# A linear-attention and mixture-of-experts kernel: the written-out order of its steps replaced by another, and more places for the experts' products among the Sinkhorn steps

## The chip, the cores and the metric

The kernel runs on one core of one Trainium2 chip. A time is the device time of one execution in microseconds (us); the figure for a kernel is the median of its runs. A profiled execution gives besides a trace, whose span runs from the first to the last instruction.

## The reference

Two computations follow one another. The first is gated linear attention over batch 4, 8 heads, 768 tokens, head size 48, in float32:

```python
for t in range(S):
    state = alpha[:, :, t, :, None] * state + np.einsum('bhd,bhe->bhde', k[:, :, t], v[:, :, t])
    y[:, :, t] = np.einsum('bhd,bhde->bhe', q[:, :, t], state)
```

Its output, as x of 3072 tokens by 384, goes through a mixture of eight experts (F = 1024) whose weights come from eight rounds of Sinkhorn normalization over all tokens:

```python
P = np.exp(logits - logits.max())          # logits = x @ w_gate
for _ in range(8):
    P /= P.sum(1, keepdims=True) + 1e-09
    P /= P.sum(0, keepdims=True) + 1e-09
    P *= N / E
for e in range(E):
    out += P[:, e:e + 1] * (np.maximum(x @ w1[e], 0.0) @ w2[e])
```

Every token's routing weight so depends on the logits of all tokens, and the Sinkhorn steps can begin only when the last chunk of attention is done. The experts' products need only x.

## The kernel before, in words

**Precision and tiles.** Each matrix of the experts is kept as two float16 parts, high and low; a product is three passes on PE, the matmul engine (lines with PASSES). In `moe_tile` a tile is T tokens (128 or 256) of one expert e: eight columns of the first layer, each of nine products into a tile `ps1` (in traces `ps<-xT,w`), evacuated by ACT (`h[0]`, ReLU) and DVE (`h[1]`, the low part); then for each 128 tokens 24 products of 128x384 (`ps<-w,h`), whose result ACT copies to `r` and SP, the queue engine, writes to DRAM as `raw`. Four PSUM buffers (psm) hold these results, so PE can run four columns ahead of the evacuation. Experts 0 to 2 are handled in this way, beside the attention; their tiles are called the filler. Experts 3 to 7 follow in a later stage with another algorithm (`first`, `second`), which starts when the filler is used up.

**Attention.** The tokens of a batch are cut into chunks of 128 and units of 256 (two chunks). The first four chunks (0 to 3, of batch 0) go through `direct_chunk`: PE transposes alpha, k and q; then for L = 1, 2, 4, 8, 16, 32, 64 small products of 32x16 and larger give the scores of level L (`psl`), DVE copies them under a mask into `A32` (rows `A<-odd,psl`), and `merge` multiplies keys and queries by decays (`T<-T,D`) and the decays among themselves (`D<-D`). This last multiplication is on DVE, or on POOL (GpSimd) where `lop[0]` is set. All other units first go through `attn_block`, which forms products of q and k of 16 tokens on POOL (`tmp_0`, `tmp_1`, ...), sums them on DVE (`AB<-tmp`), and writes the result to DRAM and back; then `attn_decays`, and `attn_chunk` for each of its two chunks (`Tk`, `Tq`, `decq`, `deck`, `psl`, `A`). Both kinds of chunk end in `attn_tail`: `psy` (the output), `pskn` and `pss` (the new state `ST`), the scaled x (`xT`) and the logits (`psg`, `lg`).

**Expert weights.** `load_expert` loads w1 and w2 of experts 0 to 2 into buffers that later hold x, ACT squares them with a sum (`w<-xT`), PE adds over partitions (`pst_w`), and ACT and DVE make the two halves; with `lop[0]` set, POOL makes the low half. `load_late` does the same for experts 3 to 7 through one staging buffer (`w1f`, then `w2f` in the same memory), a generator with a yield between its steps; the squares go to `junk`.

**Order.** The engines run the instructions in the order in which they are written (`keep_in_program_order`), PE, ACT, DVE, POOL and SP each in its own. That order is set by two strings: START for the first part of the kernel, and UNIT, which is repeated for every further unit with its numbers shifted. In them `f` emits filler worth 0.45 us of PE time (`fill`), `c3` the next step of chunk 3, `b3` the next step of the block of unit 3, `d3` its decays, `w1` the next step of loading expert 1, `g` one step for the gate's weights. A capital letter sets `lop[0]` for the step, so its multiplications go to POOL. A step that would come too early is put off (`early_`). Where there is no filler yet, `f` emits nothing.

**Sinkhorn.** `sinkhorn` is a generator. It takes the maximum of all logits (`gm` on DVE, `pst_gg` on PE, `oneg_gg` on DVE, `pso_gg` on PE, back on DVE), the exponential on ACT, and eight rounds of DVE work with one product over partitions each (`pssk`). Between its steps the caller fills in filler, and from the third step on a step of `load_late` for expert 3. The rest of the filler follows in the loop after it, with a step of `load_late` for every 2.0 us of filler as soon as no tile of expert 0 is left.

Of the kernel before, what the change touches and what calls it, by code (L numbers as in the profile page):

```python
# [25 lines left out]
def tile_gla_moe(ctx: ExitStack, tc: tile.TileContext, q, k, v, alpha, wg, w1, w2, out):  # L26
# [3 lines left out]
    E, _, FF = w1.shape  # L30
# [6 lines left out]
    NTT = NT // P  # L37
    NP = H // 2
    DP = 64
    START = 'c0 C0 f c0 f c0 c1 f c0 f C1 f f c0 f f f f f f f f f f f f f f f f f f f C0 f f f f f f f f f f f f f f f f f f f f f f f f f f f f f f f f f f f f f f f f f f f f f f f f f f f f f f f f f f f f f f f W0 f f f f f f f f f f f f f f f f C2 f f f f f f f c0 W0 f f f f f f f f f f f f f f f f f f f f f f f f f W0 f f f c1 f f f f f f f f f b2 f f f f f f f f f f f f f f f C2 f f f f f f f f f f f f f f f f f f f f f f f f f f f f f f c1 f f f f f f f f f W0 f f f f f f f f f f f f f f f f f f f f f f f f f f f f f f f f f f f f f f f f f w0 c1 f C0 f f f f f f f f f f f w0 f f f f f f f f f w0 f f f f f f f f f f C1 f w0 f f f f f f f f f f f f f f f f f f f f f f f f f f f f f f f f f f f f f f f f f f f f f f f c0 f f f f f f f f f f f f f f f f f f f f f f f f f f f f f f f f f f f f f f f f f f f f f f f f f f f f f f f f f f f f f f f f f f f f f f f f f f f f C1 f f f f f f f f f f f f f W1 f f f f f f f f f f f W1 f f f f f f f f f f f f f f f f f f f f f f f f f d2 f f f f f f f f f f f f f f W0 f f f f f f f f f f f f f f f f f f f f f f f f f f f f f f f f f f f f f f f f f f f C1 f f f f c0 f f f f f f f f f f b2 f f f f f f f f f f f f f f f f f C1 f w0 f f f f f f f f f f C2 f f f f f f f f f f f f f f f f f f f f f f f f f f B2 f f f f f f f f f f f f f f f f B3 f f f f f f f f f f f f f f f f f f f f f f f f f f f f f f f f f f f f f f f f f f f f f f f f f f f f f f f f f f f f f f f f f f c1 f f f f f f f f f f f f f f f f f f f c3 f f f f f f f f f f f f f f f C1 f f f f f f f f f f f f f f f f f f f f f f f f f f f b2 f f f f f f f f f f f f f f f f f f f f f f f f f f f f f f f f f f f f f f C2 f f f f f f g f f f f f f f f f f f f f f c0 B2 f f f f B2 f f f f f f c2 f f f f f f B2 f f f f f f f f f f f f f f f f C3 f f f f b2 f B3 f f f f f f f f c3 f f f f f f f f f f f f f f f f f W0 f f f f f f f f f b2 f f f f c1 f f f f f f f f f f f f c0 f f f f f f f f f f f f f f f f f c2 f w1 f f f f c3 f f f f f f f f f f f f f f f f f f f f f f f f f c2 f f f f f f f f f f f f f f f f f f f f f f f f f f w2 f f f f f f f f f f f f f f f c2 f f C3 f B2 f f f f f f W1 f f f f f B2 f f f f f f f f f f f f f f f f f W0 f c2 f f f f f f f f f f f f f f f f f f W0 f f f f f f f f f f f f f f f g f f f f f f f f f f f f w0 f f f f f f f f f f f f f f f f f C3 W0 f C2 f f f f f f W0 f f f f C3 f f f f f f f f f f B2 f W1 f f f f f f f f f f f f f f C3 f f f f f f f f f f f f f f C2 f f f f f f f f f f f f f f f f f f f f f f f f f f f C2 f f f f f f f f f f f f f f f f f f f f f f f f f f f f f w2 f f f f f f f f f f f f f f f f f f f f f f f f f f f f f f f f f f w2 f f f f b3 f f f f f f f f f B3 f f f b2 f f f f f f f f f f f f f f f f f f f f f f f f f d3 f f f f f C1 f f f f f b2 f f f f f f f f f f f f B2 f f f f f f f f f f W0 f f f f f f f f f f f f f f f w2 f f g f f f f f f f f f f f f f f f f f f f f f C3 f f f f f f f f f f f f f f f f f f f f f f f f f f f w1 f f f f f f f f f f f b3 f f f f f f f f f f f f w1 f f f c3 f f f c3 f f f f f f f f w1 f f f f f f f C3 f f f f f f f f f W1 f f c4 f f f f f b2 f f f f f f W1 f f f f f w1 f f f f f f f f f f W1 f f f w1 c4 f f f B3 f f B3 f f f f f f f f f f f f f f f f f f f f f f f f f f f f f f f f f f f f f f f f f f f f f f f f f f f f f f f f f f f f f f f f f f f f f f f f f f f f f f f f f f f f f w1 f f f f f f c4 f f f f f f f f f f c4 f f f f f f f f f f f f w2 f f f f c4 f f f f f f f w2 f f f f f f f f f f f f f f f f f f f f f f f f f f f f f f f f f f f f f f f f f f w2 W1 f f C2 w2 f f w2 f f f f f f f f f f f f f f f f f f f f f f f f f f f f f f f f w2 f f w1 f f f f b3 f f c3 b3 f f f f f f f f f f f f f f f c5 f f f f f f f f w2 b3 f B3 f f c6 b4 f f f f f f f B3 f b3 f f f B3 f f f f w2 f B3 f f f f f f f f f w2 c5 f f f f f f c5 f f c5 f f c4 f f f c5 f f f f w2 f f f f f f c5 f f f f f f w2 f w2 f f f w1 f f f b3 f f f b4 f f f f f f f f f f f f f f f f f B4 b4 f f f f B4 f f b4 f b4 f f f f f f B4 f f f f f f f f f f f f b4 f f f c6 B4 f f f B4 f f c6 b4 f c8 b4 f f f b4 f f f f f f b4 f c7 b5 f c6 c7 b4 f f f f c6 f f f f f f c6 f d4 f f f f f f f f f f f f f f c7 f f f c8 f c7 f f B5 c7 b5 f f f c7 f b5 f B5 B5 b5'.split()  # L40
    UNIT = 'f f f f f f f f f f f f f f f f c1 f f c0 f B1 f f f f f f f f c1 f f f f f f f f b1 f f B1 f f b1 f f b1 f f b1 f f b1 f B1 f f f f f f c0 f f B2 f f f f f f f f c1 c0 f f B1 f f c1 f c1 f f f f f d1 f f c1 f f f f f f f f f c2 f f f b2 f f f f f f c2 f f f f f f f f f f b2 b2 B2 B2 b2 f c0'.split()
    NA = 3

    pin = tc.keep_in_program_order
# [24 lines left out]
    def tr(out_, in_, idn):  # L69
# [15 lines left out]
                            fill=0.0, base=0, channel_multiplier=1)  # L85
# [46 lines left out]
    def spread(one, nm):  # L132

        n = one.shape[1]
        ps = psa.tile([P, 512], F32, tag="psa", name=f"pso_{nm}")
        mm(ps[:, :n], ones[0:1, :], one)
        g = sm.tile([P, n], F32, tag=f"all{n}", name=f"all_{nm}")
        VE.tensor_copy(g, ps[:, :n])
        return [g[:, i:i + 1] for i in range(n)]
# [594 lines left out]
    def fill(us):  # L734
        owed[0] += us
        while owed[0] > 0 and filler:
            e, gen, n = filler[0]
            if n == FT and e not in ready:
                break
            try:  # L740
                owed[0] -= next(gen)
                filler[0][2] += 1
            except StopIteration:
                filler.pop(0)
        owed[0] = min(owed[0], 0.0)
# [124 lines left out]
    def sinkhorn():  # L870
        gm = sm.tile([P, 1], F32, tag="gm", name="gm")
        VE.tensor_reduce(gm, lg, axis=AX.XY, op=ALU.max)
        gg, = spread(top(gm, None, "gg"), "gg")
        lm = mp.tile([P, NTT, E], F32, tag="lm", name="lm")
        VE.tensor_scalar(lm, lg, gg, None, op0=ALU.subtract)
        SE.activation(PR, lm, AF.Exp)
        for it in range(N_SINKHORN):
            rs = sm.tile([P, NTT], F32, tag="rs", name=f"rs_{it}")
            VE.tensor_reduce(rs, PR, axis=AX.X, op=ALU.add)
            VE.tensor_scalar_add(rs, rs, EPS)  # L880
            ri = sm.tile([P, NTT], F32, tag="ri", name=f"ri_{it}")
            VE.reciprocal(ri, rs)
            VE.tensor_mul(PR, PR, ri.unsqueeze(2).to_broadcast([P, NTT, E]))
            yield
            ps = psa.tile([P, 512], F32, tag="psa", name=f"pssk_{it}")
            mm(ps[:, :NTT * E], ones, PR.rearrange("p t e -> p (t e)"))
            cs = sm.tile([P, E], F32, tag="cs", name=f"cs_{it}")
            VE.tensor_reduce(cs, ps[:, :NTT * E].rearrange("p (t e) -> p e t", e=E), axis=AX.X, op=ALU.add)

            VE.tensor_scalar(cs, cs, EPS, float(E) / NT, op0=ALU.add, op1=ALU.mult)  # L890
            ci = sm.tile([P, E], F32, tag="ci", name=f"ci_{it}")
            VE.reciprocal(ci, cs)
            VE.tensor_mul(PR, PR, ci.unsqueeze(1).to_broadcast([P, NTT, E]))
        VE.tensor_mul(PR, PR, p2t.unsqueeze(2).to_broadcast([P, NTT, E]))
# [93 lines left out]
    filler[1:] = sorted(filler[1:], key=lambda x: x[0])  # L988
    w3_ = load_late(NA)
    advance(w3_, 1)  # L990
    for n, _ in enumerate(sinkhorn()):
        fill(2.8 if n else 4.0)
        if n > 1:
            advance(w3_, 1)
    while filler:
        if all(e for e, *_ in filler):
            advance(w3_, 1)
        fill(2.0)
    advance(w3_, 99)
    early.close()  # L1000
    attn_ps.close()
# [161 lines left out]
```

## Time and profile before

| | us |
|---|---|
| median of 3 runs | 1732.25 (1730.5 to 1732.73) |
| profiled execution, device time | 1735.68 |
| its span, first to last instruction | 1734.0 |

The mean granted clock of PE in the profiled execution is 0.975. The program has 46403 instructions, 19984 of them matmuls. In rows of a timeline the first number is the start in us from the start of the span, the second the duration, and a bracket gives the idle time of the engine before it and what ended that. A row with xN merges N neighbouring instructions of the same kind; its duration is then from the first start to the last end or the sum, short waits included. PE, DVE, ACT, POOL and SPq name the engines (SPq is SP's queue of DMA issues).

### The profile page before, as it was taken

How to read it: one execution, taken by the hardware profiler on the slowest of the kernel's cores; microseconds unless marked ns; L12 is line 12 of the kernel's file. 1: busy time of each engine (PE TensorE's matmuls, PEld its weight loads, DVE VectorE, ACT ScalarE, POOL GpSimd, SP SyncE). 2: the span in 40 equal slices, each digit the busy share in tenths (PEclk: the TensorE clock that was granted, in tenths of full speed). 3: DMA queues.
4: the chain of work that ended last, by engine and by line, in shares of the span. 5: the costliest groups of instructions: out<-in, count | busy, mean ns of one | idle time of the engine just before them, and what ended most of it. 6: DMA issues, size and time to landing. Idle time of an engine off the chain costs nothing.

```text
span 1734.0 us, 46403 instructions
## 1 busy us (share of the span) xinstructions
PE 1650.9 (95%) x19984; PEld 1420.5 (82%) x19984; DVE 1221.1 (70%) x2992; ACT 796.8 (46%) x1592; POOL 290.9 (17%) x262
## 2 busy tenths in 40 slices
PE   5679999999999999999999999999999999999999
PEld 4556767777777777776899999999999999999998
DVE  5767767666656766355577878888788867786666
ACT  3456433334333434334465545554555445544443
POOL 2424245435533633000000000000000000000000
PEclk7679999999999999999999999999999999999999
DMA  7153422442243133021202020202020201000001
GB/s 178 37 124 87 105 63 60 100 100 61 59 101 89 48 90 73 24 61 55 69 24 70 29 65 25 69 28 58 28 65 29 51 2 38 2 1 20 29 29 38
DMA packets 149501, 98.91 MB, mean 57 GB/s; under 512 B 108464, under 2 KB 139440, under 8 KB 149296
## 3 DMA queue, kind: packets, MB, share of 16 engines
q1 hardware_dynamic: 149296, 95.95, 21.2%
q8 instruction: 156, 2.56, 0.6%
q14 instruction: 49, 0.40, 0.1%
HBM read 67.63 MB, written 28.30 MB: 55 GB/s over the span
## 4 chain that ended last, share of the span: by engine, by line
PE 78%; DVE 15%; ACT 3%; issue 2%; POOL 1%; DMA 1%; SPq 0%; ACTq 0%; DVEq 0%; POOLq 0%
PE ps L67 49%; PE ps2x L67 12%; PE ps2v L67 3%; PE ps2z L67 3%; DVE h L58 3%; PE ps2y L67 3%; PE psy L67 2%; PE psl L67 2%; DVE hf L58 2%; DVE w L58 1%; ACT h L58 1%; DVE acc L58 1%; DVE decq L58 1%; DVE AB L58 1%; DVE deck L58 1%
## 5 line engine op out<-in xcount | busy, mean ns | idle before, releaser
L67 PE MATMUL ps<-xT,w 128*128 128x256 f16 (+1 forms) x6984 | 806.9, 273 | 16.2 <-DVE h L58 11.5
L67 PEld LDWEIGHTS <-w 128*128 128x128 f16 x6984 | 676.5, 98 | 99.4 <-issue 18.4
L67 PEld LDWEIGHTS <-h 128*128 128x128 f16 x6768 | 588.0, 98 | 118.4 <-issue 9.4
L58 ACT CAST h<-hf 128x896 f16<-128x896 f32 x240 | 224.8, 937 | 337.6 <-DVE hf L58 227.6
L58 DVE TENSOR_TENSOR h<-hf,h 128x896 f16<-128x896 f32 x240 | 261.5, 1089 | 165.5 <-ACT h L58 164.0
L67 PE MATMUL ps<-w,h 128*128 128x384 f16 x1728 | 297.1, 327 | 0.5 <-DVE h L58 0.4
L67 PE MATMUL ps2x<-w,h 128*128 128x192 f16 x2880 | 267.7, 246 | 7.6 <-DVE ps2z L58 5.5
L58 DVE TENSOR_TENSOR hf<-hf 128x128 f32<-128x128 f32 x960 | 235.3, 286 | 39.5 <-ACT hf L58 30.8
L58 DVE SCALAR_TENSOR_TENSOR h<-ps,h 128x256 f16<-128x256 f32 (+1 forms) x296 | 115.6, 411 | 140.9 <-ACT h L58 140.3
L58 ACT ACTIVATE h<-ps 128x256 f16<-128x256 f32 (+1 forms) x296 | 110.3, 377 | 164.1 <-PE ps L67 164.1
L58 ACT ACTIVATE hf<-ps 128x512 f32<-128x512 f32 x240 | 142.4, 593 | 54.1 <-PE ps L67 54.1
L58 POOL TENSOR_TENSOR tmp<-qt,kt 128x768 f32<-128x768 f32 (+1 forms) x80 | 133.2, 1670 | 126.9 <-DVE qt L58 72.7
L58 ACT COPY r<-ps 128x384 f32<-128x384 f32 x72 | 34.4, 479 | 158.5 <-PE ps L67 144.1
L58 DVE TENSOR_REDUCE AB<-tmp 128x16 f32<-128x768 f32 (+2 forms) x90 | 80.7, 903 | 33.5 <-POOL tmp L58 33.3
L67 PE MATMUL ps2v<-w,h 128*128 128x192 f16 x720 | 70.2, 248 | 0.0
L58 ACT COPY A<-psl 16x128 f32<-16x128 f32 (+3 forms) x164 | 52.5, 327 | 37.5 <-PE psl L67 25.3
L67 PE MATMUL ps2y<-w,h 128*128 128x192 f16 x720 | 69.2, 246 | 0.0
L67 PE MATMUL ps2z<-w,h 128*128 128x192 f16 x720 | 69.2, 246 | 0.0
L58 DVE SCALAR_TENSOR_TENSOR acc<-ps2x,pe,acc 128x192 f32<-128x192 f32 x120 | 49.2, 410 | 1.8 <-PE ps2x L67 1.8
L67 PE MATMUL psl<-T 48*32 48x16 f32 (+2 forms) x1472 | 24.1, 219 | 27.4 <-DVE T L58 10.9
L67 PEld LDWEIGHTS psl<-T 48*32 48x32 f32 (+1 forms) x1472 | 20.7, 139 | 31.8 <-DVE T L58 12.4
L58 ACT ACTIVATE w<-w2f,s_w 128x768 f16<-128x768 f32 x35 | 32.6, 933 | 30.5 <-DVE w2f L58 29.1
(186 smaller groups left out, 1325.5 us busy)
## 6 DMA issues: line engine op xcount, KB each, us to landing
raw<-r SPq DMA_DIRECT2D x72, 192.0 KB, 1.9
ri<-raw SPq DMA_DIRECT2D x72, 192.0 KB, 2.4
w1f<-in_moe_w_dram SPq DMA_DIRECT2D x20, 384.0 KB, 7.0
w2f<-in_moe_w_dram SPq DMA_DIRECT2D x5, 1536.0 KB, 7.0
VN<-in_v_dram SPq DMA_DIRECT2D x48, 96.0 KB, 3.0
xT<-in_moe_w_dram SPq DMA_DIRECT2D x6, 768.0 KB, 4.6
out_dram<-acc SPq DMA_DIRECT2D x24, 192.0 KB, 2.0
qt<-in_q_dram SPq DMA_DIRECT2D x10, 384.0 KB, 4.7
```

Source lines behind the costliest of these rows:

```text
L58: r = f(*a, **k_)
L67: tc.keep_in_program_order(nc.tensor.matmul(out_, lhsT, rhs, start=start, stop=stop, **k_))
```

## The change

Two things are replaced. First, both strings START and UNIT. The new START has 1972 steps where the old one has 1996, the new UNIT 131 where the old one has 132; the steps of chunks, blocks, decays and weights are the same in number, the number of `f` differs (1783 and 1807, 102 and 103), and which of them are capitals changes. According to its author the order was found by a planner that now takes PE's clock at the front as half. Second, the Sinkhorn generator yields the amount of filler that it wants, has two more yields in its first part, and the loop behind it takes 2.4 instead of 2.0 us of filler per step. The number of yields before the steps of `load_late` set in is raised by the two, so these begin in the same round.

```diff
-    START = 'c0 C0 f c0 f c0 c1 f c0 f C1 f f c0 f f f
...
-    UNIT = 'f f f f f f f f f f f f f f f f c1 f f c0 f B1 f f
...
+    START = 'c0 C0 C0 C0 f C1 f c0 f f f f f f f f C1 f f f
...
+    UNIT = 'f f f f f f f f f f f f f f c1 f f c0 f f f f f f f B1
...
         VE.tensor_reduce(gm, lg, axis=AX.XY, op=ALU.max)
-        gg, = spread(top(gm, None, "gg"), "gg")
+        yield 1.2
+        one = top(gm, None, "gg")
+        yield 0.8
+        gg, = spread(one, "gg")
...
             VE.tensor_mul(PR, PR, ri.unsqueeze(2).to_broadcast([P, NTT, E]))
-            yield
+            yield 2.8 if it else 4.0
...
-    for n, _ in enumerate(sinkhorn()):
-        fill(2.8 if n else 4.0)
-        if n > 1:
+    for n, us in enumerate(sinkhorn()):
+        fill(us)
+        if n > 3:
             advance(w3_, 1)
     while filler:
         if all(e for e, *_ in filler):
             advance(w3_, 1)
-        fill(2.0)
+        fill(2.4)
```

Three places show what moves. The first is ACT behind the Sinkhorn rounds. `r_22` and `r_23` are copies of the second layer's results of the tile of expert 1 at token 2816, `h_2_2560` the evacuations of the next tile, `junk,w2m` the squares of expert 3's w2, which wait for the load of `w2f`. Before:

```order
L58 COPY r_22_11483<-ps_1_2816_0_11456 128x384
L58 COPY r_23_11514<-ps_1_2816_1_11489 128x384
L58 ACTIVATE junk,w2m_11517<-w2f_11487 128x768 x2
L58 ACTIVATE h_2_2560_11520<-ps_2_2560_0_11522 128x256
L58 ACTIVATE h_2_2560_11520<-ps_2_2560_1_11534 128x256
L58 ACTIVATE junk,w2m_11517<-w2f_11487 128x768 x2
L58 ACTIVATE h_2_2560_11520<-ps_2_2560_2_11548 128x256
```

And now:

```order
L58 COPY r_22_11483<-ps_1_2816_0_11456 128x384
L58 COPY r_23_11514<-ps_1_2816_1_11486 128x384
L58 ACTIVATE h_2_2560_11517<-ps_2_2560_0_11519 128x256
L58 ACTIVATE h_2_2560_11517<-ps_2_2560_1_11531 128x256
L58 ACTIVATE junk,w2m_11543<-w2f_11494 128x768 x2
L58 ACTIVATE h_2_2560_11517<-ps_2_2560_2_11546 128x256
L58 ACTIVATE h_2_2560_11517<-ps_2_2560_3_11558 128x256
```

The first two evacuations of the tile now stand ahead of the squares. On PE, 24 products of the tile of expert 1 at token 2560 that stood behind `pso_gg` now stand ahead of `pst_gg` or between the two.

The second place is POOL in a repeated unit, at chunk 2 of batch 2. `deck`, `A` and `Tk` belong to the chunk, `tmp_2_2_..` to the block of a later unit. Before:

```order
L58 TENSOR_TENSOR ST_119<-ST_120,dtot_0_5649 48x4x48 x2
L58 TENSOR_TENSOR deck_2_2_6621<-Tk_2_6606,suf_130 128x256
L58 TENSOR_TENSOR A_2_6623<-an_1_6438,mask 128x8x8x16
L58 TENSOR_TENSOR tmp_2_2_54_6649<-qt_2_6454,kt_2_6455 128x768
L58 TENSOR_TENSOR Tk_2_6606<-Tk_2_6606,k_2_1_6525 128x512
L58 TENSOR_TENSOR tmp_2_2_55_6786<-qt_2_6454,kt_2_6455 128x384
```

And now:

```order
L58 TENSOR_TENSOR ST_119<-ST_120,dtot_0_5647 48x4x48 x2
L58 TENSOR_TENSOR deck_2_2_6567<-Tk_2_6552,suf_130 128x256
L58 TENSOR_TENSOR A_2_6569<-an_1_6219,mask 128x8x8x16
L58 TENSOR_TENSOR Tk_2_6552<-Tk_2_6552,k_2_1_6523 128x512
L58 TENSOR_TENSOR tmp_2_2_54_6776<-qt_2_6383,kt_2_6384 128x768
L58 TENSOR_TENSOR tmp_2_2_55_6799<-qt_2_6383,kt_2_6384 128x384
```

The first product of the block has moved behind `Tk`, which may start only after the chunk's `psl` on PE has read the old value.

The third place is DVE in the front, from the first scores of chunk 2 (`A_0_2`) to x of chunk 0 (`xT_0`), on which the first tile of filler waits. `AB_123` are the sums of the block of unit 2, `qt_2` and `al_2` its merges. Before:

```order
L58 TENSOR_TENSOR A_0_2_945<-psl_2_912,same 128x256
L58 TENSOR_TENSOR T_2_768<-T_2_768,D_0_2_766 128x2x256
L58 TENSOR_REDUCE AB_123<-tmp_0_2_0_894 128x16
L58 TENSOR_TENSOR qt_2_587<-qt_2_587,al_2_589 128x768
L58 COPY_PREDICATED A_0_2_945<-odd,psl_2_912 128x128
L58 TENSOR_TENSOR T_2_768<-T_2_768,D_0_2_979 128x2x128x2
L58 TENSOR_REDUCE wgm<-wgf 128x1
L58 TENSOR_TENSOR xT_0_82<-ys_0_879,xT_0_79 128x3x128
```

And now, from the first sum of the block on:

```order
L58 TENSOR_REDUCE AB_123<-tmp_0_2_0_822 128x16
L58 TENSOR_TENSOR T_1_368<-T_1_368,D_0_1_884 128x2x4x64
L58 TENSOR_TENSOR qt_2_475<-qt_2_475,al_2_477 128x768
L58 TENSOR_REDUCE wgm<-wgf 128x1
L58 TENSOR_REDUCE AB_123<-tmp_0_2_1_1026 128x8
L58 TENSOR_TENSOR qt_2_475<-qt_2_475,al_2_477 128x8x48
L58 TENSOR_TENSOR al_2_477<-al_2_477 128x8x48
L58 TENSOR_REDUCE AB_123<-tmp_0_2_2_1034 128x4x2
L58 COPY_PREDICATED A_0_2_928<-odd,psl_2_895 128x128
L58 TENSOR_TENSOR D_0_2_1072<-D_0_2_962 128x128
L58 TENSOR_TENSOR T_2_768<-T_2_768,D_0_2_962 128x2x128x2
L58 TENSOR_TENSOR xT_0_82<-ys_0_831,xT_0_79 128x3x128
```

Two more sums of the block and the merges between them have moved ahead of chunk 2's second level and of `xT_0`. Its loads (`qt`, `al`, `kt`) are issued ahead of those of chunk 2 where they stood behind them. Among the D merges of `merge`, POOL now has the first two of chunk 0 and of chunk 3 (128x256 and 128x128) and the first of chunk 1, where it had those of chunk 2.

More of the change, by code (lines that the diff above doesn't have):

```diff
@@ L42, in tile_gla_moe @@
+    UNIT = 'f f f f f f f f f f f f f f c1 f f c0 f f f f f f f B1 f f f f f b1 f f f f f f f B1 f f f f b1 B1 f f b1 f f B1 b1 f f b1 f f f f f c0 f c1 f f f f f f B2 c1 f f f f f f c0 f f c1 f f f f f d1 f f f f c1 c2 f f f f f f f f c1 f f f f c2 c0 f f f f f f f f b2 f f f f f B2 f b2 f B2 f B2 b2'.split()
     NA = 3
```

3 lines of the change are left out of this document (1 added, 2 removed).

## The prediction, made before the changed kernel ran

> **What bounds the kernel now.** I read the page first, then the busy time by stage, then PE's waits by stage, and last the timelines at the places where those waits stand. The page says that PE, the matmul engine, is busy for 95% of the span:
>
> ```profile
> span 1734.0 us, 46403 instructions
> PE 1650.9 (95%) x19984; PEld 1420.5 (82%) x19984; DVE 1221.1 (70%) x2992; ACT 796.8 (46%) x1592; POOL 290.9 (17%) x262
> ```
>
> So the end can only move by what PE idles and by what it does at a lowered clock. The table by stage (columns: length, busy time and instructions of PE, of its weight loads, of DVE, ACT and POOL; then granted clock, DMA share, GB/s) says where that is:
>
> ```profile
> 0.00:130.00 130.00, 80.74 (x2308) 64.49 (x2309) 82.41 (x193) 55.81 (x127) 41.38 (x70) 0.73 0.47 113
> 130.00:330.00 200.00, 187.84 (x2416) 142.63 (x2416) 141.65 (x268) 93.66 (x241) 84.50 (x66) 0.99 0.35 88
> 330.00:740.00 410.00, 405.84 (x5274) 310.00 (x5267) 255.38 (x496) 155.07 (x420) 165.01 (x127) 1.00 0.28 69
> 740.00:840.00 100.00, 94.12 (x718) 70.97 (x717) 54.75 (x149) 39.44 (x83) 0.00 (x0) 0.98 0.27 73
> 840.00:1734.00 894.00, 882.41 (x9292) 832.38 (x9289) 686.93 (x1889) 452.87 (x723) 0.00 (x0) 1.00 0.12 35
> ```
>
> The front, up to 130 us, has 49.3 us of PE idle time (130 less 80.74) at a mean clock of 0.73. The next 200 us have 12.2 us idle, the repeated units (330 to 740) 4.2 us, the Sinkhorn stage (740 to 840) 5.9 us at 0.98, and the rest 11.6 us. The rest is code that the change does not touch. PE's work itself is the same products in another order, so the four earlier stages hold all that can be gained.
>
> What PE waits for in the front (total us, times, longest):
>
> ```profile
> PE psl L67 <- DVE T L58: 10.9, 7, 3.8
> PE psl L67 <- DVE A L58: 8.2, 7, 2.0
> PE psl L67 <- issue: 6.7, 3, 3.8
> ```
>
> These are the chunk chains: DVE's merges (T) and masked copies (A), each of which PE's next small products need. The 6.7 us put down to "issue" are waits for nothing that the profile shows, and I expect the change to leave them. In the repeated units little is left:
>
> ```profile
> PE psl L67 <- DVE decq L58: 2.5, 5, 0.5
> PE ps L67 <- DVE h L58: 1.7, 1, 1.7
> ```
>
> **The Sinkhorn stage.** It has four waits that I can name:
>
> ```profile
> PE ps L67 <- DVE h L58: 2.8, 1, 2.8
> ...
> PE pssk L67 <- DVE PR L58: 1.0, 1, 1.0
> PE pst_gg L70 <- DVE gm L58: 1.0, 1, 1.0
> ...
> PE pso_gg L67 <- DVE oneg_gg L58: 0.4, 1, 0.4
> ```
>
> The first Sinkhorn steps run in series: DVE's maximum gm, PE's transposition of it, DVE's maximum of that, PE's spreading. In the program before, nothing stands between them on PE. The two new yields let `fill` put products there: in the new order 24 products of the experts stand ahead of pst_gg, and six between it and pso_gg. At 0.11 us or more each (4.09 us for 36 smaller ones, in a row below) six take at least 0.68 us and cover the 0.37; so 0.96 + 0.37 = 1.33 us go. The 1.03 us in front of the last pssk go too: there PE has two columns of nine products between two pssk before, and three now, while DVE's chain between them is unchanged.
>
> The largest item is the wait of 2.76 us for h. Its cause is not DVE. PE's own rows (idle time in brackets):
>
> ```profile
> 793.61 4.09 PE L67 MATMUL ps<-xT,w 128*128 128x256 f16 x36
> 800.47 5.76 PE L67 MATMUL ps<-xT,w 128*128 128x256 f16 x36 [2.76 <-DVE h L58]
> ```
>
> ACT's row just ahead of it, and the queue's row of the load for which ACT waits:
>
> ```profile
> 797.78 0.84 ACT L58 ACTIVATE junk<-w2f 128x768 f16<-128x768 f32 x1 [3.44 <-DMA w2f<-in_moe_w_dram]
> ```
>
> ```profile
> 790.93 0.38 SPq L58 DMA_DIRECT2D w2f<-in_moe_w_dram  x1
> ```
>
> ACT runs in order. It reached the squares of the w2 load at 794.34, the load issued at 790.93 released them only at 797.78, and h stood behind them. PE ran on until its four buffers were full. Besides that, the 36 products after the wait took 5.76 us where the 36 before it took 4.09, and the clock fell:
>
> ```profile
> 800.00:803.00 3.00, 2.53 (x16) 1.96 (x16) 1.42 (x5) 2.81 (x8) 0.00 (x0) 0.71 0.00 0
> ```
>
> The loss is 2.76 + (5.76 - 4.09) = 4.43 us. With 2.4 in place of 2.0 us per step, the squares come two evacuations of h later (the ACT rows in the section on the change); the load is released by the same DVE work as before and lands at the same place. By hand: PE then has two more columns of about 1.02 us (4.09 / 4) before it blocks, so 2.76 shrinks to about 0.8, a second short wait of some 0.4 follows behind the other two squares, and an idle time that short should keep the clock. I take 1.2 us left and 3.2 gained. Sum of the stage: 1.33 + 1.0 + 3.2 = **5.5 us**; bounds 2.4 (the load's wait merely moves) and 6.8 (all four gone).
>
> **The repeated units.** In each one PE waits 0.50 us for decq:
>
> ```profile
> 449.29 0.68 PE L67 MATMUL psl<-decq,deck 48*64 48x64 f32 x16 [0.50 <-DVE decq L58]
> ```
>
> The cause stands on POOL and DVE:
>
> ```profile
> 446.87 1.99 POOL L58 TENSOR_TENSOR tmp<-qt,kt 128x768 f32<-128x768 f32 x1
> ```
>
> ```profile
> 447.12 2.02 DVE L58 TENSOR_TENSOR decq<-Tq,pre 128x256 f32<-128x256 f32 x1
> ```
>
> DVE's decq of 128x256 began at 447.12 and took 2.02 us, ending with POOL's tmp that began at 446.87 and ended at 448.86. In the new unit POOL's product Tk, which waits for the psl group itself, stands ahead of that tmp, so nothing is on POOL when decq runs. Also twelve products more stand between PE's transposition and psl, so decq is early anyway. Of 2.5 + 1.7 = 4.2 us I take **3.3**; all of it is the lower bound of the time. The upper bound is no gain: psy of the unit's second chunk now follows its psl after three columns (about 3.1 us), while ACT's copies of A alone take
>
> ```profile
> 450.06 2.40 ACT L58 COPY A<-psl 64x512 f32<-64x512 f32 x7 [1.77 <-POOL Tk L58]
> ```
>
> 2.40 us, and a late evacuation ahead of them would put a new 0.5 us wait in place of the old one.
>
> **From 130 to 330 us** the new START shifts most steps by a column or two. Of the 12.2 us I see no single wait that must go; the groups that wait there (h, the square sums of weights, xT) keep their neighbours. I take **1.0 us**, with half of the idle time gone (6) and a third more (4 slower) as bounds.
>
> **The front.** From the first merge of chunk 2 after the first tile to PE's psy of chunk 2, DVE is the chain. These are DVE's rows that the new order moves out of that stretch:
>
> ```profile
> 69.54 0.45 DVE L58 COPY_PREDICATED A<-odd,psl 128x128 f32<-128x128 int32 x1
> ...
> 70.51 0.53 DVE L58 TENSOR_REDUCE AB<-tmp 128x8 f32<-128x384 f32 x1
> 70.97 0.54 DVE L58 TENSOR_TENSOR qt<-qt,al 128x384 f32<-128x384 f32 x1
> 71.54 0.36 DVE L58 TENSOR_TENSOR al<-al 128x192 f32<-128x192 f32 x1
> ...
> 73.62 0.95 DVE L58 TENSOR_REDUCE AB<-tmp 128x16 f32<-128x768 f32 x1 [0.87 <-POOL tmp L58]
> ...
> 74.88 1.87 DVE L58 TENSOR_TENSOR D<-D 128x256 f32<-128x256 f32 x1
> ...
> 87.86 1.74 DVE L58 TENSOR_REDUCE AB<-tmp 128x32 f32<-128x1536 f32 x1
> ```
>
> and its end on PE:
>
> ```profile
> 91.14 1.51 PE L67 MATMUL psy<-T,ST 128*32 128x128 f32 x24 [1.33 <-DVE T L58]
> ```
>
> The block's reductions AB of tmp_3 and tmp_4 with qt and al (0.53 + 0.54 + 0.36 + 0.95) now stand before it, the large AB (1.74) behind it, and chunk 3's first D merge (1.87) is on POOL: 6.0 us less between 69.54 and 91.14. The price is ahead of it: xT of the first tile now stands behind AB of tmp_0 to tmp_2 on DVE, which wait for POOL's products. POOL's prices in the front:
>
> ```profile
> L58 POOL TENSOR_TENSOR tmp<-qt,kt 128x768 f32<-128x768 f32 x5 | 9.8, 1961 | 8.7 <-DVE AB L58 6.2 <-DVE qt L58 2.5
> ...
> L58 POOL TENSOR_TENSOR kt<-kt,al 128x384 f32<-128x384 f32 x4 | 4.1, 1014 | 0.3
> ...
> L58 POOL TENSOR_TENSOR tmp<-qt,kt 128x384 f32<-128x384 f32 x3 | 3.3, 1119 | 8.5 <-DVE qt L58 8.5
> ...
> L58 POOL TENSOR_TENSOR D<-D 128x256 f32<-128x256 f32 x1 | 0.6, 603 | 0.0
> ...
> L58 POOL TENSOR_TENSOR D<-D 128x128 f32<-128x128 f32 x1 | 0.4, 400 | 0.0
> ```
>
> Of the serial pair tmp_1 and tmp_2 with the kt between them, 1.12 + 1.01 + 1.12 = 3.25 us can be exposed; the DVE work itself fills idle time there. What queues behind these waits on DVE are chunk 2's masked copy and merge, xT, and all evacuations of the first tile, for which PE waits. Net -6.0 + 3.3 = **-2.7 us**. The bounds are -6.0 with the waits hidden, and those of the rivals.
>
> One row shows what a merge on POOL can cost. DVE's D merge at 74.88 lasted to 76.75, while this product of POOL lasted to 76.47:
>
> ```profile
> 74.65 1.82 POOL L58 TENSOR_TENSOR tmp<-qt,kt 128x768 f32<-128x768 f32 x1 [0.18 <-DVE AB L58]
> ```
>
> Alone it needs no more than the 0.28 us left. The Trainium skill, SBUF — State Buffer, section "SBUF: two separate sides", has this as a rule: the port pair shared by VectorE and GpSimd is an exclusive lock, held for a whole instruction, among others against a VectorE operation with two SBUF inputs. The trace agrees in that row (1.87 us). By that rule the larger merges that START gives to POOL are not free, which is the second case below.
>
> **The sum.** 5.5 + 3.3 + 1.0 + 2.7 = 12.5 us. The profiled execution took 1735.68 us for its span of 1734.0, the runs have a median of 1732.25; I subtract from both. 1735.68 - 12.5 = 1723.2 for the like of the profiled execution, and **1719.8** for the median. About 0.2%, or 3.5 us, is what a measurement of this kernel can tell from no change: 1728.8 and 1735.7 are the marks.
>
> **The rivals.**
> - *The forecast*, 1719.8, chance 0.55.
> - *POOL holds the front.* The merges that POOL takes over (two of 128x256, one of 128x128 more: 2 x 0.60 + 0.40 = 1.6 us) and tmp_3 and tmp_4 (1.12 + 1.96) are exposed as well: 4.7 us, so the front costs 2.0 us and the sum is 9.8 - 2.0 = 7.8: 1724.5; with the middle at its slow bound 1729 to 1733. For it: the row above. Against it: DVE stands idle in that part for 3.5 us. Chance 0.20, of which 0.12 within 0.2%.
> - *Slower: the first tile stalls.* All of tmp_0 to tmp_4 and both kt are exposed in front of xT and h: 2 x 1.96 + 3 x 1.12 + 2 x 1.01 = 9.3 us, the stretch to psy gets no shorter since PE's own latency takes the place of what left, and PE's idling keeps the clock down for two more windows like this one, 2.5 us lost in each:
>
> ```profile
> 80.00:85.00 5.00, 0.84 (x64) 0.73 (x64) 5.00 (x14) 0.00 (x0) 1.64 (x2) 0.50 0.00 0
> ```
>
> That is 14.3 us, against 9.8 from the other stages: 4.5 slower, 1736.8. It decides from 13.3 us on. Against it: the block's loads are issued earlier now, so tmp_0 can start earlier. Chance 0.12.
> - *The front's clock rises.* PE's work there is 80.74 x 0.73 = 59 us at full clock; at 0.80 it takes 73.7, 7 us less, of which half may be on the chain. With the full 6.0 us: 9.8 + 6.0 + 3.5 = 19.3, or 1713.0. Chance 0.13. The Trainium skill, TensorE: Matmul & The Clock Gate, Part 1, states that about 3.4 us without work in a free-running window halves the clock; the row with PE busy 0.84 of 5 us at clock 0.50 agrees.
>
> That the change does nothing is ruled out by the order rows.
>
> **The numbers.** Faster by over 0.2%: 0.55 + 0.13 + 0.08 = 0.76; within: 0.12; slower: 0.12. The range runs from 1709, the last case with part of the middle's gain, to 1733, the second with the middle's loss.
>
> **What would show it.** Right: no wait of pst_gg, pso_gg or the last pssk; the wait for h behind the w2 load under 1.3 us at clock 1.00; no 0.50 us wait for decq in the units; psy of chunk 2 before 89 us. Wrong: a wait of PE for h or xT in the first tile over 5 us, DVE rows beside POOL's of twice their length in the front, or a new wait of psy for ACT's A in every unit.

## The result, and the profile after

The changed kernel took 1719.13 us (median of 4 runs, 1718.25 to 1721.49) where the kernel before took 1732.49 (4 runs, 1730.5 to 1734.55). The ratio is 0.9924, with a 95% interval of 0.9912 to 0.9936: 13.4 us faster, where 12.5 were forecast (1719.8). The profiled execution took 1718.25 us, 0.9 below its median; that of before lay 3.2 above its own (1735.68), so some 4 of the 17.5 us between the two spans (1734.0 and 1716.5) are no part of the change.

The same stages in the table of windows:

```profile
0.00:130.00 130.00, 87.48 (x2362) 71.17 (x2363) 74.81 (x200) 59.96 (x136) 41.89 (x70) 0.71 0.50 121
130.00:330.00 200.00, 190.52 (x2501) 144.11 (x2499) 142.19 (x279) 92.57 (x243) 91.23 (x71) 1.00 0.33 84
330.00:740.00 410.00, 404.48 (x5220) 310.95 (x5219) 249.05 (x491) 152.10 (x417) 150.25 (x122) 1.00 0.30 73
740.00:840.00 100.00, 95.28 (x759) 73.47 (x758) 61.92 (x172) 45.09 (x89) 0.00 (x0) 1.00 0.22 62
```

What PE loses in a stage is its idle time and the time at a lowered clock. From 130 to 330 us it idled 12.2 us before and 9.5 now, and a window at half clock that cost 1.6 us before is gone: some 4.3 us. From 330 to 740 us, in the repeated units, it idled 4.2 us before and 5.5 now; against this stand 1.7 us that a window at half clock cost before (0.66 from 510 to 515 us; over 410 us that is too little to show in a clock rounded to 1.00). So nothing that can be told was gained.

The Sinkhorn stage can't be read from these windows. They are fixed in time, and pst_gg starts at 753.53 us before and at 740.23 us now, so the last window now reaches the first two waits of the last phase (1.34 and 0.79 us), which it did not before. The waits that the prediction named and the half clock behind the w2 load came to 6.8 us before (0.96 + 0.37 + 1.03 + 2.76 + 1.67); what stands in their place now comes to 1.6 (0.75 + 0.61 + 0.21). That is 5.2 us in these two executions.

So the total came out as forecast and the parts did not: the stage for which 1.0 us was taken gave some 4, and the units, with 3.3, gave nothing. The profile says why in the units; PE's largest wait from 330 to 740 us:

```profile
PE psy L67 <- DVE Tq L58: 4.6, 6, 1.6
```

The five waits of 0.50 us for decq and the one of 1.66 us for h are gone, and a new one of psy for DVE's Tq stands six times in their place. In the Sinkhorn stage, PE's rows:

```profile
740.23 0.27 PE L70 MATMUL pst_gg<-ident,gm 128*1 128x128 f32 x1
...
741.41 0.38 PE L67 MATMUL pso_gg<-oneg_gg,ones 1*128 1x1 f32 x2
...
759.48 0.56 PE L67 MATMUL pssk<-PR,ones 128*128 128x192 f32 x2 [0.75 <-DVE PR L58]
...
787.51 2.12 PE L67 MATMUL ps<-xT,w 128*128 128x256 f16 x18 [0.61 <-DVE h L58]
789.85 4.06 PE L67 MATMUL ps<-w,h 128*128 128x384 f16 x24 [0.21 <-DVE h L58]
```

pst_gg and pso_gg wait for nothing, the wait for h behind the w2 load is 0.61 + 0.21 instead of 2.76 us, and the 18 products behind it take 2.12 us, the full clock. The wait at the last pssk is gone, but one of 0.75 us stands at the fifth. In the front:

```profile
52.47 1.51 PE L67 MATMUL psy<-T,ST 128*32 128x128 f32 x24 [1.20 <-DVE T L58]
...
60.18 5.56 PE L67 MATMUL ps<-xT,w 128*128 128x128 f16 x71 [1.96 <-DVE xT L58]
...
83.44 1.51 PE L67 MATMUL psy<-T,ST 128*32 128x128 f32 x24
```

psy of chunk 2 starts at 83.44 us (91.14 before), ahead of the 89 that the prediction set as a mark. That mark tells little, since executions differ by some 3 us ahead of it: with the old START and the Sinkhorn edits psy of chunk 2 starts at 88.29 us too. From psy of chunk 1 to that of chunk 2 are 31.0 us now and 35.5 before. The first tile waits 1.96 us for xT and nowhere for h.

### The profile page after: what moved, and what is told of

It is laid out like the page before. It is cut to its first block, busy times and chain, and to the rows that moved or that the text cites. A ratio compares the mean times of both kernels' runs of the same rounds, so it can differ in the third digit from the quotient of the medians.

```text
span 1716.5 us, 46368 instructions
## 1 busy us (share of the span) xinstructions
PE 1644.9 (96%) x19984; PEld 1418.4 (83%) x19984; DVE 1203.2 (70%) x2993; ACT 793.8 (46%) x1592; POOL 283.4 (17%) x261
## 4 chain that ended last, share of the span: by engine, by line
PE 74%; DVE 17%; ACT 4%; issue 2%; POOL 2%; DMA 1%; SPq 0%; ACTq 0%; DVEq 0%; POOLq 0%
PE ps L67 46%; PE ps2x L67 12%; DVE h L58 4%; PE ps2z L67 3%; PE ps2v L67 3%; PE ps2y L67 3%; DVE hf L58 2%; PE psy L67 2%; DVE AB L58 2%; PE psl L67 2%; POOL tmp L58 2%; DVE tmp L58 2%; ACT h L58 2%; DVE w L58 1%; ACT w L58 1%
## 5 line engine op out<-in xcount | busy, mean ns | idle before, releaser
L58 POOL TENSOR_TENSOR tmp<-qt,kt 128x768 f32<-128x768 f32 (+1 forms) x80 | 125.1, 1568 | 161.0 <-DVE AB L58 87.0
L67 PEld LDWEIGHTS psl<-T 48*32 48x32 f32 (+1 forms) x1472 | 20.2, 132 | 27.7 <-DVE A L58 12.9
```

Of the source, the lines that this page charges most:

```text
L58: r = f(*a, **k_)
L67: tc.keep_in_program_order(nc.tensor.matmul(out_, lhsT, rhs, start=start, stop=stop, **k_))
```

## The experiments

Each kernel but the change itself was timed against the kernel before in five rounds. The last column is the median less that of the kernel before in the same rounds.

| kernel | us (median) | ratio to before, 95% interval | us against before |
|---|---|---|---|
| the change | 1719.13 | 0.9924 (0.9912 to 0.9936) | -13.4 |
| Sinkhorn edits alone | 1728.14 | 0.9973 (0.9964 to 0.9982) | -4.2 |
| START alone | 1728.45 | 0.9975 (0.9966 to 0.9984) | -3.9 |
| UNIT alone | 1740.61 | 1.0043 (1.0030 to 1.0055) | +8.3 |
| the change with 2.0 in the loop | 1722.25 | 0.9935 (0.9922 to 0.9947) | -10.1 |
| START and UNIT | 1722.46 | 0.9940 (0.9924 to 0.9955) | -10.4 |
| front of START alone | 1732.39 | 0.9996 (0.9986 to 1.0006) | -0.5 |
| the change, no merges of START on POOL | 1720.53 | 0.9927 (0.9914 to 0.9941) | -12.3 |
| the change, psy of the unit later | 1715.17 | 0.9896 (0.9881 to 0.9910) | -17.7 |
| rest of START, and UNIT | 1723.32 | 0.9940 (0.9928 to 0.9952) | -9.6 |
| 2.4 in the loop alone | 1729.66 | 0.9979 (0.9969 to 0.9988) | -3.3 |
| the change without the two yields | 1721.16 | 0.9927 (0.9915 to 0.9940) | -11.8 |
| the change, psy later, 3.2 and 2.8 us | 1720.01 | 0.9922 (0.9910 to 0.9934) | -12.9 |

**The Sinkhorn edits alone**: the lines of the diff below UNIT, with both strings as before.

> The kernel before with the Sinkhorn edits alone (the yields with their amounts, n > 3, 2.4 us per step); START and UNIT as before. Theory (the stages add up): the waits of pst_gg, pso_gg go (0.96 + 0.37), the wait for h behind the w2 load shrinks from 2.76 to about 0.8 us and the products behind it keep the full clock (1.7 us), one pssk wait of some 0.8 us stays: 5.2 us faster, 1727. Rival (the time at half clock isn't bought by a wait but comes back at another place): only idle time is gained, 3.5 us or less, 1728.7 or later. Second rival (the stage's gain hangs on where the new START and UNIT leave the filler): under 2 us.

4.2 us faster (interval 3.1 to 6.2), between the theory's 5.2 and the first rival's 3.5; it doesn't decide between them. The trace has the wait behind the w2 load at 1.84 us instead of 2.76, and the time behind it at full clock:

```profile
798.19 6.01 PE L67 MATMUL ps<-w,h 128*128 128x384 f16 x36 [1.84 <-DVE h L58]
```

All waits for pssk together are 0.2 us, less than the 0.8 that was expected. What follows: the edits work behind the old order too, with a larger remainder of the wait for h.

**2.4 in the loop alone.**

```diff
-        fill(2.0)
+        fill(2.4)
```

> The kernel before with 2.4 us per step in the loop behind the Sinkhorn steps, and nothing else changed. Theory of the prediction: the wait of 2.76 us for h shrinks to about 1.2 us or less and its half clock goes, 3.2 us faster, 1729.3. Rival (the lowered clock follows such a wait in only a part of the executions): 1.6 to 2.4 us faster, 1730 to 1730.8.

3.3 us faster (interval 2.1 to 5.4): the 3.2 of the prediction, and its 1.2 us of remaining wait, 1.01 + 0.21:

```profile
798.88 2.12 PE L67 MATMUL ps<-xT,w 128*128 128x256 f16 x18 [1.01 <-DVE h L58]
801.22 4.06 PE L67 MATMUL ps<-w,h 128*128 128x384 f16 x24 [0.21 <-DVE h L58]
```

**The change with 2.0 in the loop**, the same line turned back.

> The changed kernel with 2.0 us per step again in the loop behind the Sinkhorn steps (instead of 2.4). Theory: ACT's squares of the w2 load stand two evacuations of h earlier again, PE's wait for h behind them grows from 0.8 to about 2.8 us and the products behind it run at half clock for 3.4 us: 3.5 to 3.7 us slower than the changed kernel, 1722.7. Rival (the earlier load, not the two columns, took the wait away): the wait stays under 1.5 us and the time within 1 us of the changed kernel, 1719 to 1720.

1722.25, as the theory had it, though the ratios of the two overlap. The trace shows half of the mechanism: the wait is back, but the 18 products behind it took 2.12 us, so this execution (1718.24, the fastest of the five, and as fast as the change) kept the clock; that others lose it there is not shown in the new order:

```profile
785.51 2.12 PE L67 MATMUL ps<-xT,w 128*128 128x256 f16 x18 [2.09 <-DVE h L58]
```

**The change without the two yields.**

```diff
-        yield 1.2
...
-        yield 0.8
...
-        if n > 3:
+        if n > 1:
```

> The changed kernel without the two new yields at the first steps of the Sinkhorn phase (and n > 1 again, so that the loads stay at their steps). Theory: the waits of pst_gg and pso_gg are back, 1.33 us slower than the changed kernel, 1720.4. Rival (DVE's chain behind them starts later, so the waits are only moved to the first pssk): no difference, 1719.1.

2.0 us slower by the medians (1.6 against each one's own runs of before), but the intervals overlap, so the time alone doesn't decide. The trace does, in part:

```profile
739.56 0.38 PE L67 MATMUL pso_gg<-oneg_gg,ones 1*128 1x1 f32 x2 [0.37 <-DVE oneg_gg L58]
...
754.10 0.56 PE L67 MATMUL pssk<-PR,ones 128*128 128x192 f32 x2 [0.90 <-DVE PR L58]
```

The first row is back as forecast, and the fifth pssk waits 0.90 us instead of 0.75. But pst_gg doesn't wait here: the new strings alone put its cover in place, so of the forecast's 1.33 us the yields buy some 0.4 to 0.5.

**START alone.**

```diff
-    START = 'c0 C0 f c0 f c0 c1 f c0 f C1 f f c0 f f f
...
+    START = 'c0 C0 C0 C0 f C1 f c0 f f f f f f f f C1 f f f
...
```

> The kernel before with the new START alone; UNIT and the Sinkhorn edits as before. Theory of the prediction: front 2.7 and 130 to 330 us 1.0, so 3.7 faster: 1728.8. What the two profiles suggest instead: idle time and time at half clock together fell by 2.7 us up to 130 us and by 5.5 us from there to 330 us, so 8 faster: 1724. Rival (POOL holds the front): 2 us or less faster. The idle stretch of 1.66 us at 509 us with its 3.4 us at half clock and the five waits of 0.50 us for decq stay.

3.9 us faster, at the forecast's 3.7. But this agrees for the wrong reason, as the trace shows: a new stall behind the last unit takes part of a larger gain.

```profile
674.45 0.58 PE L70 MATMUL psd<-ident,DN 16*128 16x16 f32 x4 [4.34 <-DMA DN<-ds]
```

**UNIT alone.**

```diff
-    UNIT = 'f f f f f f f f f f f f f f f f c1 f f c0 f B1 f f
...
+    UNIT = 'f f f f f f f f f f f f f f c1 f f c0 f f f f f f f B1
...
```

> The kernel before with the new UNIT alone. Theory of the prediction: 3.3 us faster, 1729. What the profile of the changed kernel suggests: the five waits for decq and the one for h (2.5 + 1.7 us, and 1.7 us at half clock behind the latter) go, but psy of each unit's second chunk waits for DVE's Tq instead (4.6 us in six): 0 to 1.5 us faster, 1731 to 1732.5. Rival (behind the old START the new order meets other fill levels): slower by up to 2 us.

8.3 us slower, beyond all that was expected. The waits for decq are gone, and a wait for h of 2.39 us stands in four units, one of 1.45 in the last; PE's waits for h from 330 to 740 us:

```profile
PE ps L67 <- DVE h L58: 11.4, 6, 2.4
```

The old and the new START have as many steps of chunks and blocks, but START's number of f differs by 24, at most 10.8 us of filler; so another part of a tile stands next to each step of UNIT, and each unit repeats it. (That it is this is argued; no run shifts the filler alone.) A string so has no price of its own: -3.9 and +8.3 alone, -10.4 together.

**START and UNIT**, both as above, and the Sinkhorn part as before.

> The kernel before with the new START and the new UNIT together; the Sinkhorn edits as before. Theory (two independent parts: the pair of strings, and the Sinkhorn edits): 13.2 less the 4.2 that the Sinkhorn edits gave alone, so 9 us faster than before, 1723.3; no wait of 4.3 us for the load DN at 670 us as with the new START alone, no waits of 2.39 us for h as with the new UNIT alone. Rival (each part hangs on the fill that the others leave): more than 2 us away from that.

10.4 us faster (interval 7.8 to 13.2), in reach of the theory's 9, and neither of the two stalls is there. With the 4.2 of the Sinkhorn edits the sum is 14.6, against 13.4 for all. pst_gg waits for nothing here, while with START alone its wait of 1.0 us stands: the pair of strings covers it without the yields.

**Front of START alone**, up to the place where both strings have done the same 84 steps (some 107 us), and **the rest of START, and UNIT**, its complement; the first:

```diff
-    START = 'c0 C0 f c0 f c0 c1 f c0 f C1 f f c0 f f f
...
+    START = 'c0 C0 C0 C0 f C1 f c0 f f f f f f f f C1 f f f
...
```

> The kernel before with only the front of START new: up to the place where both strings have done the same 84 steps (PE at chunk 3's psl_3 of the first half, some 107 us), then the old START, UNIT and Sinkhorn part. Theory of the prediction: the front is worth 2.7 us, 1729.7, and the waits from 130 us on stay as before. The two profiles suggest up to 5.9 us for it, 1726.5, with psy of chunk 2 at 83.4 us instead of 91.1. Rival (what the front gains is given back behind it, where the old order meets another fill): within 1.5 us of before, 1731 to 1733.

> The kernel before with the old START up to the place where both strings have done the same 84 steps (some 107 us), and from there the new START and the new UNIT; Sinkhorn edits as before. The complement of the front alone. Theory (the new order's gain lies behind 107 us: less idle time and half clock from 130 to 330 us, some 5 us in every profile with the new START, and an end of the units without the stall of the mixed kernels): 8 to 10 us faster than before, 1723 to 1725, that is within 2.5 us of the two strings together (1722.5). Theory of the prediction (front 2.7, 130 to 330 us 1.0, units 3.3): 4.3 us faster, 1728.5.

The front alone gives 0.5 us (interval 2.4 faster to 1.0 slower), its complement 9.6. PE's rows in the front's trace, from psy of chunk 0 to the first row of dense products:

```profile
36.88 1.93 PE L67 MATMUL psy<-A,VN 128*32 128x128 f32 x32
...
50.51 0.71 PE L67 MATMUL psl<-T 48*32 48x32 f32 x28 [2.93 <-DVE A L58]
...
55.56 1.51 PE L67 MATMUL psy<-T,ST 128*32 128x128 f32 x24 [1.20 <-DVE T L58]
...
86.49 1.51 PE L67 MATMUL psy<-T,ST 128*32 128x128 f32 x24
...
96.04 0.97 PE L67 MATMUL ps<-w,h 128*128 128x384 f16 x5 [1.28 <-POOL w L58]
...
123.77 9.33 PE L67 MATMUL ps<-xT,w 128*128 128x256 f16 x71 [1.48 <-DVE xT L58]
```

And the same of before (psy of chunk 2 there stands at 91.14):

```profile
38.34 1.93 PE L67 MATMUL psy<-A,VN 128*32 128x128 f32 x32
...
49.09 0.78 PE L67 MATMUL psl<-T 48*32 48x32 f32 x32 [1.63 <-DVE A L58]
...
55.66 1.51 PE L67 MATMUL psy<-T,ST 128*32 128x128 f32 x24
...
126.30 4.00 PE L67 MATMUL ps<-xT,w 128*128 128x256 f16 x18 [1.48 <-DVE xT L58]
```

From psy of chunk 1 to that of chunk 2 are 30.9 us (35.5 before): 4.5 us gained. Around this stretch most of it is given back. From psy of chunk 0 to that of chunk 1 are 18.7 us (17.3), because PE waits 2.93 us for the masked copy of chunk 1's scores, where it waited 1.63: DVE now does the end of chunk 0 (m, st, ys, pw) and 1.02 us of a weight matrix ahead of that copy. From psy of chunk 2 to the dense products are 37.3 us (35.2): the first tile's second layer now comes to the halves of w2 before they are there, and PE waits 0.48 us for DVE's and 1.28 us for POOL's. In all, the dense products begin 86.9 us behind psy of chunk 0 and began after 88.0: 1.1 us gained. The wait of 2.9 us for A and the two for the weights' halves stand in every trace with the new front, and in none with the old.

**The change, no merges of START on POOL**: its 27 capital C made small.

> The changed kernel with all merges of START on DVE (its 27 capital C steps made small, so that POOL's 12 products of D are on DVE). Theory of the forecast (POOL's merges take work off DVE's chain): the 12 rows come back on DVE, at 0.2 to 0.6 us each 3 to 4 us in all, about half of it on the chain: 1 to 3 us slower than the changed kernel, 1720 to 1722. Rival (POOL holds the front, and its merges make DVE's rows long): 1 to 3 us faster, 1716 to 1718.

1720.53, 1.4 us slower by the medians, and not told apart by the ratios (0.9927 and 0.9924). As far as the merges go the rival is out: they don't hold the front. Nor do they bring much; the largest costs DVE 0.42 us here, with POOL idle, where the prediction counted 1.87 as saved and took 0.28 for it alone:

```profile
78.33 0.42 DVE L58 TENSOR_TENSOR D<-D 128x256 f32<-128x256 f32 x1
```

**The change, psy of the unit later.**

```diff
-... c0 f c1 f f f f f f B2 c1 f f f f f f c0 ...
+... c0 f c1 f f f f f f B2 f f f c1 f f f c0 ...
```

> The changed kernel with one step of UNIT three f later, the psy of the unit's second chunk (one column of nine products more between psl and psy). Theory (psy's wait for DVE's Tq, 4.6 us in six, is what ate the gain of the units): five of the six waits go and the one of 1.55 us shrinks to 0.5, so 3.5 to 4 us faster than the changed kernel, 1715.5. Rival (DVE's row of h and Tq behind the block's sums is late as a whole, so the wait moves to the next product that needs h, or to ACT's ab): under 1 us faster, 1718.5 to 1719.5.

1715.17, 4.0 us faster than the change; the intervals (0.9881 to 0.9910 and 0.9912 to 0.9936) don't overlap. From 330 to 740 us the wait for Tq is gone, and this one is the largest:

```profile
PE ps L67 <- DVE h L58: 1.8, 3, 0.7
```

So the wait for Tq took what the units could have gained, and one column of nine products hides it. This is the fastest kernel of the study.

**The change, psy later, 3.2 and 2.8 us.**

```diff
-            yield 2.8 if it else 4.0
+            yield 3.2 if it else 4.0
...
-        fill(2.4)
+        fill(2.8)
```

(and UNIT as in the last)

> The changed kernel with the step of UNIT three f later (as in the run with psy later), and with 3.2 instead of 2.8 us at each Sinkhorn round and 2.8 instead of 2.4 us in the loop behind. Theory: the run with psy later gave 1715.2; the wait of 0.75 us at the fifth pssk and the two of 0.61 and 0.21 us for h go as well: 1713.6. Rival (the filler used up earlier is missed at the later rounds and at the change to the last phase): 1715 to 1717.

1720.01, 4.8 us slower than without these two edits: the rival's direction, and beyond its 1717. The waits at pssk and those of 0.6 and 0.2 us for h are gone, and new ones for ACT stand behind, of 1.13 us at h and of 0.96 us at hf where the last phase begins:

```profile
790.37 4.69 PE L67 MATMUL ps<-w,h 128*128 128x384 f16 x27 [1.13 <-ACT h L58]
```

```profile
740.00:840.00 100.00, 93.72 (x733) 72.17 (x732) 62.05 (x170) 45.28 (x88) 0.00 (x0) 0.98 0.22 62
```

In this window PE does 93.72 x 0.98 = 91.8 us of work, 3.4 less than the 95.3 of the change. With more filler for each step of the weights fewer of these steps fit before the filler ends, and the rest is done in one go where the last phase begins; that this is what makes ACT late there is argued. The rest of the 4.8 us wasn't traced; between the two profiled executions 1.9 us stand ahead of the first dense products, where the order is the same.

## Why the prediction was right, and where it wasn't

The time, the direction and the Sinkhorn mechanism were right. Three of the four terms were badly sized, and their errors cancelled: that the sum fell within 0.9 us of the result is luck.

**Sinkhorn, 5.5 us forecast.** 4.2 alone, and 3.0 as the step from both strings (10.4) to all (13.4); by the waits of the two profiles 5.2, of which 1.67 is time at half clock, which doesn't come in every execution. The w2 term held (3.2 forecast, 3.3 measured with an interval of 2.1 to 5.4, 1.2 us of wait left as forecast). The 1.0 for the last pssk went, but "three now, while DVE's chain between them is unchanged" was read off the last round alone: in the change the fifth has twelve products ahead of it and waits 0.75 us. And 0.96 of the 1.33 us for pst_gg was won by the strings.

**The units, 3.3 us forecast, nothing measured.** The failed step is the 3.3 taken of 4.2 us: the new wait of psy wasn't counted in, though the very place, psy three columns behind psl, was named with its upper bound of no gain. It was named for ACT's copies of A, and what came late was DVE's Tq. DVE's rows of the changed kernel, and PE's:

```profile
471.33 0.95 DVE L58 TENSOR_REDUCE AB<-tmp 128x16 f32<-128x768 f32 x1 [1.92 <-POOL tmp L58]
...
476.35 0.71 DVE L58 TENSOR_TENSOR Tq<-Tq,q 128x512 f32<-128x512 f32 x1
```

```profile
477.12 0.86 PE L67 MATMUL psy<-Tq,ST 128*32 128x128 f32 x24 [1.09 <-DVE Tq L58]
```

DVE waits 1.92 us for a product of the block on POOL; h, m, ys, ST and Tq are queued behind it. POOL's product is late in turn because it waits for DVE's sums of the large product of the block, which took 3.37 us:

```profile
463.40 3.37 DVE L58 TENSOR_TENSOR tmp<-qt,kt 128x1536 f32<-128x1536 f32 x1
```

```profile
469.49 1.81 POOL L58 TENSOR_TENSOR tmp<-qt,kt 128x768 f32<-128x768 f32 x1 [4.34 <-DVE AB L58]
```

The first half of the mechanism held: decq no longer meets POOL. But that large product of DVE now does, every time. The groups by form from 130 to 740 us, before:

```profile
L58 DVE TENSOR_TENSOR decq<-Tq,pre 128x256 f32<-128x256 f32 x20 | 23.2, 1161 | 0.0
L58 DVE TENSOR_TENSOR tmp<-qt,kt 128x1536 f32<-128x1536 f32 x9 | 22.2, 2466 | 0.0
```

and after:

```profile
L58 DVE TENSOR_TENSOR tmp<-qt,kt 128x1536 f32<-128x1536 f32 x9 | 30.3, 3366 | 0.0
...
L58 DVE TENSOR_TENSOR decq<-Tq,pre 128x256 f32<-128x256 f32 x20 | 13.9, 694 | 0.0
```

decq gained 9.3 us of DVE time and tmp lost 8.1: the collision moved. One of them, with POOL's row beside it:

```profile
227.08 3.37 DVE L58 TENSOR_TENSOR tmp<-qt,kt 128x1536 f32<-128x1536 f32 x1
```

```profile
227.01 1.81 POOL L58 TENSOR_TENSOR tmp<-qt,kt 128x768 f32<-128x768 f32 x1 [0.83 <-DVE qt L58]
```

Before, where POOL stood idle, the same product took 1.75 us; 3.37 is that, begun where POOL ended:

```profile
79.69 1.75 DVE L58 TENSOR_TENSOR tmp<-qt,kt 128x1536 f32<-128x1536 f32 x1
```

The 1.6 us more is as long as the longest of PE's waits for Tq, so the collision is enough to make them; that it does is argued, since no run takes it away. The Trainium skill, SBUF — State Buffer, section "SBUF: two separate sides", has it as an exclusive lock for a whole instruction; the trace agrees (3.37 us, and 1.75 us alone).

**130 to 330 us, 1.0 us forecast, some 4.3 in the profiles.** The failed step is "I see no single wait that must go". PE waited 5.1 us for h there, in four rows, and waits 2.1 now, at most 0.60 in one. Two of the rows of before:

```profile
181.68 2.13 PE L67 MATMUL ps<-xT,w 128*128 128x256 f16 x18 [1.80 <-DVE h L58]
...
240.29 2.13 PE L67 MATMUL ps<-xT,w 128*128 128x256 f16 x18 [1.70 <-DVE h L58]
```

Their cause stood in DVE's and POOL's rows, which weren't read. At the first:

```profile
176.98 2.03 DVE L58 TENSOR_TENSOR decq<-Tq,q 128x256 f32<-128x256 f32 x1
```

```profile
176.84 1.89 POOL L58 TENSOR_TENSOR A<-an,mask 128x1024 f32<-128x1024 f32 x1
```

The next decay, deck, began at 178.94 and took 2.02 us beside a product of POOL, where a decay of this size without POOL beside it took 0.41 (decq at 180.88). Two decays of DVE, each locked out by POOL, hold four evacuations. At the second it is the large product:

```profile
236.53 3.37 DVE L58 TENSOR_TENSOR tmp<-qt,kt 128x1536 f32<-128x1536 f32 x1
```

```profile
236.45 1.83 POOL L58 TENSOR_TENSOR tmp<-qt,kt 128x768 f32<-128x768 f32 x1
```

In the new order the collisions are still there, but not where PE waits long for the evacuations behind them. The 1.6 us at half clock are not a second gain of their own: before, 30 products behind a wait for the weights' squares took 6.66 us, but in the trace of the front alone, in the same order, they took 5.04, and PE then stood longer at h, with 18 products behind it that took 3.79 us instead of 2.13:

```profile
166.46 6.66 PE L67 MATMUL ps<-w,h 128*128 128x384 f16 x30
```

```profile
162.43 5.04 PE L67 MATMUL ps<-w,h 128*128 128x384 f16 x30
...
177.70 3.79 PE L67 MATMUL ps<-xT,w 128*128 128x256 f16 x18 [2.77 <-DVE h L58]
```

From the start of the 30 products to the end of the wait for h are 15.2 us before and 15.3 in the front alone: DVE sets the time there, whether PE's clock falls or not. The traces of the Sinkhorn edits alone and of 2.4 in the loop alone, with the old START, have the wait of 2.77 us as well. The complement of the front (9.6 us faster) shows that most of the change lies behind the first 107 us; how it divides rests on the profiles alone, and the 4.3 us here with the 0.96 of pst_gg are not all of it.

**The front, 2.7 us forecast, 0.5 to 0.8 measured** (0.5 alone, and 10.4 less 9.6 as the difference of both strings to its complement, each to some 2 us). The chain from psy of chunk 1 to that of chunk 2 did get shorter, by 4.5 us, since the moved rows weighed more than the exposed products. The failed step is "Net -6.0 + 3.3 = -2.7 us", which takes the gain of this one stretch for that of the front: PE's longer wait for chunk 1's copy A ahead of it (1.4 us later) and its waits for the halves of w2 behind it (1.8 us) weren't counted, and some 1 us was left.

**The rivals.** POOL's merges do not hold the front (with them off it is not faster). The first tile does not stall (1.96 us at xT, no wait for h). The front's clock did not rise (0.73 before and 0.71 now in the tables of windows, though that record can be wrong, see below).

## What to carry to other kernels

Read the engine behind each wait: a wait of PE for an evacuation was a collision of two other engines, three rows up. Measure a chain from a mark that the change doesn't move to one behind all that it moves: the stretch that was made shorter showed 4.5 us, the whole front 1.1. A step moved to where it hides one wait shows its price at the next engine that queues behind it, so the order of every queue around the step is to be read, not only the one with the wait. And parts of an order that were found together have no price apart: the sum of parts may be right by chance, so test them alone and together.

## What the runs showed of the hardware

**The half clock behind a short wait comes in some executions only.** Before, a column of nine products 3.2 us behind a wait of 1.66 us took 2.07 us; with the Sinkhorn edits alone, where everything up to there is in the same order, the wait was 1.65 and the column took 1.16:

```profile
509.43 1.14 PE L67 MATMUL ps<-xT,w 128*128 128x256 f16 x9 [1.66 <-DVE h L58]
...
512.62 2.07 PE L67 MATMUL ps<-xT,w 128*128 128x256 f16 x9
```

```profile
508.04 1.14 PE L67 MATMUL ps<-xT,w 128*128 128x256 f16 x9 [1.65 <-DVE h L58]
...
510.65 1.16 PE L67 MATMUL ps<-xT,w 128*128 128x256 f16 x9
```

In START alone a wait of 2.72 us at the w2 load kept the clock as well (the 18 products at 796.80 us took 2.12), where before's of 2.76 lost it.

The Trainium skill, TensorE: Matmul & The Clock Gate, Part 1, speaks of an idle window of some 3.4 us that runs freely; waits about half as long lowered the clock here in some executions. Whether one does may hang on where in such a window it falls; no run here shows that. It may be one reason why runs of one kernel scatter over 3 to 4 us, and a single profile is no measure of such a term.

**The clock's record can be wrong.** In START alone the window from 40 to 50 us reads 1.00, yet four transpositions at 41.16 us take 1.12 us, and four like them at 69.99 us 0.66. Durations of like products are the surer sign. **The front itself scatters**: with the same START, psy of chunk 1 starts at 52.47 us in the change and at 56.19 in START alone, and PE's waits in the front that are put down to nothing that the profile shows add up to 4.3 and 7.2 us.
